# A spectral layer and two MLPs on one core: when weight conversions and low parts are made, and two-bank tiles in the inverse transform

## The chip, the cores and the metric

One core of one Trainium2 chip runs the whole program. The metric is the device time in microseconds (us). The kernel before took 1181.35 us, the median of three runs (1181.19, 1181.35 and 1182.56). Engines are named as in the profile: PE is TensorE, PEld its weight loads, DVE VectorE, ACT ScalarE, POOL GpSimd, SP SyncE.

## The reference

Inputs are `x` (2, 3008, 256) in float32, two 256x256 mixing matrices, two biases, and the float64-valued weights of two MLPs (256 to 2048 to 256).

```python
X = np.fft.rfft(x, axis=1);  Xr, Xi = X.real, X.imag
Yr = Xr @ w_r - Xi @ w_i + b_r
Yi = Xr @ w_i + Xi @ w_r + b_i
Y* = sign(Y*) * max(abs(Y*) - 0.01, 0)          # on Yr and on Yi
y = np.fft.irfft(Yr + 1j*Yi, n=3008, axis=1)    # then reshaped to 6016 tokens
h = y @ w_in;  g = h / (1 + exp(-1.702 h));  y = g @ w_out     # first MLP
h = y @ w_in2; g = h / (1 + exp(-h));        y = g @ w_out2    # second MLP
```

## The kernel before

The program has four stages, told apart on PE: the forward transform (to 67.3 us of the profiled execution), the mixing (to 140.41), the inverse transform (to 197.59) and the MLPs (the rest). The transforms are matmuls with tables that are loaded from HBM (`load_m`, L111); the MLPs are a seven-product scheme with each product in three passes over high and low parts.

**The mixing** has 12 units, one for each (b, p, j), that is batch, half of the spectrum and block of 128 frequencies (`mids`). `mid_mm` (L492) does the matmuls of a unit into two PSUM tiles `psm`, `mid_post` takes the sums, differences and the threshold on DVE and ACT, `mid_fold` makes the tiles `f` (and `fd`) that the inverse reads. Units 0 and 1 (`n32` = 2) are plain float32 matmuls. Units 2 to 11 split both operands in a high and a low part and do 25 matmuls each: for each of eight groups the passes `wh,xh`, `wl,xh`, `wh,xl`, and once the bias. The high part `xh` is a cast on ACT (L480). The low part `xl` is made in two steps (`xsplit`, L468): ACT writes the rounded negative (L476), then POOL issues a DMA that adds the value `xt` to it (L477, 256 KB each, two for a unit). The low parts have 8 buffers and are ordered four units ahead of their use (`xsplit(i + 4, 1)`).

**The weight conversions.** The MLP weights come as 64-bit words. A call of `tick` (L251) moves a chain of blocks on by one: POOL issues an accumulating DMA `cv_a<-cv_c` for the last block's bits (L227); for the block before that, four sums on DVE (L202 to L205, `tmp`), a cast on ACT (L99) and two subtractions on POOL (L100) place it as `wi` (or `wo`, without sums); for a new block, ACT takes the absolute value of `raw` (L165) and DVE does five bit operations (L170 to L174, `cv_c`); then SP loads the next `raw`, which has a single buffer. So L174 of a block is followed by the accumulating DMA, and that by the sums of the same block on DVE, which wait until it has landed. The first ticks stand in the forward loop (`tf`), others in the mixing behind units 2, 6 and 10 (`tm`) and in the inverse behind steps 1, 4, 7 and 10 (`ti`).

**The inverse** has 16 steps (q, b, t), four for each of four output blocks. In `inv_mm` (L567) each step writes two PSUM banks `psi`, one for each half of the channels, taken one by one from the same two pools of four banks that the other stages use. `inv_post` (L600) empties them: for t = 0 and 1, into `rt` (for q = 0 by an ACT copy L611 of one bank and DVE sums L619 and L374, for q = 1 by ACT copies L606), for t = 2 and 3 by a sum into `ac` (L627) and a difference into `rt` (L628), both on DVE. `inv_out` (L636) then combines `ac` and `rt` into the tokens `yt` (L644, L648). `ac` and `rt` have one buffer each.

Engines run their instructions in program order. In nearly all places that order is worked out when the program is built, by a scheduler that looks at dependencies and at due times of its own; only a few engines of some stages keep the order of the code (POOL and SP in the forward transform, SP in the mixing, PE in the inverse).

Of the kernel before, what the change touches and what calls it, by code (L numbers as in the profile page):

```python
# [17 lines left out]
ALU = mybir.AluOpType  # L18
# [38 lines left out]
def spectral_mlp_kernel(ctx, tc, xin, mfwd, minv, wc, bias, w_in1, w_out1, w_in2, w_out2, outT):  # L57
# [408 lines left out]
    xsp = {}  # L466

    def xsplit(i, part):  # L468
        if not N('n32') <= i < len(mids):
            return  # L470
        b, p, j = mids[i]
        for cs in range(2):
            x = xt[b, p, j, cs].rearrange("p q m c -> p (q m c)")
            if part:
# [560 lines left out]
```

## Time and profile before

| | |
|---|---|
| median of three runs | 1181.35 us |
| the profiled execution | 1181.88 us, span 1179.8 us |
| mean granted TensorE clock | 0.998 |
| PE busy | 1157.4 us (98% of the span) |
| ACT, DVE, POOL busy | 761.3, 632.7, 499.9 us |
| stages on PE | forward to 67.3, mixing to 140.4, inverse to 197.6, MLPs to the end |

The profiled execution is 0.53 us above the median. PE is busy in 98% of the span, and the page's slices show the granted clock at nine tenths or more throughout, so what a change can give or cost is in single waits of PE. The view of waits names them, and the timeline of PE says where each stands. Times in rows are microseconds from the start of the span.

### The profile page before, as it was taken

The page shows a single profiled execution, that of the slowest core. Times are in us where ns is not written, and L with a number is a line of the kernel's source. Part 1 is how long each engine was busy: PE and PEld are TensorE (multiplying, and loading weights), DVE is VectorE, ACT ScalarE, POOL GpSimd, SP SyncE. Part 2 cuts the span into 40 slices and gives each one's busy share as a digit, 9 for nine tenths or more (in the row PEclk, how much of TensorE's full clock was granted, in tenths as well). Part 3 has the DMA queues.
Part 4 walks back from the last instruction along what each step waited for, and adds up shares of the span by engine and source line. Part 5 has one row for each costly group of instructions (what it writes and reads, how often), then busy time and mean ns, then how long its engine had stood idle before and what let it go on. Part 6 is the DMA issues. An engine that isn't in the chain of part 4 may idle for free.

```text
span 1179.8 us, 14452 instructions
## 1 busy us (share of the span) xinstructions
PE 1157.4 (98%) x5036; PEld 940.4 (80%) x5036; DVE 632.7 (54%) x976; ACT 761.3 (65%) x1437; POOL 499.9 (42%) x421
## 2 busy tenths in 40 slices
PE   7999989999999999999999999999999999999998
PEld 4758866788888888888889978878888888888897
DVE  7857998666456465565564553432532623524422
ACT  2465633678667667677667776666765765766655
POOL 2353532454444444444436755333333333433333
PEclk9999999999999999999999999999999999999999
DMA  7568332231221221121120100000000000000000
GB/s 267 181 135 229 54 72 54 55 80 28 54 72 36 54 72 28 45 72 37 54 63 28 54 18 19 1 37 1 1 37 1 20 17 1 36 1 1 36 1 32
DMA packets 33610, 61.35 MB, mean 52 GB/s; under 512 B 3073, under 2 KB 12289, under 8 KB 33538
## 3 DMA queue, kind: packets, MB, share of 16 engines
q1 hardware_dynamic: 25730, 46.28, 11.6%
q0 software_dynamic: 7808, 14.16, 6.9%
q8 instruction: 39, 0.64, 0.2%
q14 instruction: 33, 0.27, 0.1%
HBM read 35.92 MB, written 10.35 MB: 39 GB/s over the span
## 4 chain that ended last, share of the span: by engine, by line
PE 72%; ACT 5%; DVE 2%; issue 1%; DMA 0%; POOL 0%; DVEq 0%; ACTq 0%; POOLq 0%
PE o L727 38%; PE x L755 34%; ACT yt L758 2%; ACT g L760 1%; ACT x L674 1%; DVE x L681 1%; ACT yt L774 0%; DVE yt L776 0%; DVE yt L731 0%; DVE yt L797 0%; ACT yt L791 0%; DMA cv_a<-cv_c 0%; ACT yt L789 0%; ACT yt L731 0%; ACT wi L99 0%
## 5 line engine op out<-in xcount | busy, mean ns | idle before, releaser
L765 POOL TENSOR_TENSOR g<-yt,g 128x512 fp32r<-128x512 f32 (+1 forms) x282 | 361.3, 1294 | 531.6 <-PE x L755 364.3
L727 PE MATMUL o<-g,wo 128*128 128x512 f32 (+1 forms) x2304 | 561.0, 386 | 0.9 <-POOL g L765 0.9
L755 PE MATMUL x<-x,wi 128*128 128x512 f32 (+1 forms) x2016 | 501.7, 387 | 5.4 <-ACT yt L791 2.0
L727 PEld LDWEIGHTS o<-g,wo 128*128 128x128 f32 x2304 | 432.4, 188 | 83.6 <-POOL g L765 1.2
L755 PEld LDWEIGHTS x<-x,wi 128*128 128x128 f32 x2016 | 376.0, 188 | 86.0 <-ACT yt L774 5.6
L758 ACT ACTIVATE yt<-yt 128x512 f32<-128x512 f32 (+1 forms) x288 | 179.1, 622 | 257.8 <-DVE yt L797 209.9
L760 ACT CAST g<-yt 128x512 fp32r<-128x512 f32 (+1 forms) x384 | 234.4, 612 | 11.8
L797 DVE TENSOR_TENSOR yt<-yt,x 128x512 f32<-128x512 f32 (+1 forms) x96 | 64.7, 674 | 212.9 <-PE x L755 212.6
L776 DVE TENSOR_TENSOR yt<-yt,x 128x512 f32<-128x512 f32 (+1 forms) x96 | 64.8, 675 | 168.7 <-ACT yt L774 165.9
L765 DVE TENSOR_TENSOR g<-yt,g 128x512 fp32r<-128x512 f32 (+1 forms) x102 | 72.7, 713 | 77.8 <-ACT g L760 77.8
L344 PE MATMUL psf<-m,xf 128*128 128x376 f32 (+2 forms) x208 | 61.1, 456 | 6.4 <-DVE xf L303 6.1
L681 DVE TENSOR_TENSOR x<-yt,x 128x512 fp32r<-128x512 f32 (+1 forms) x46 | 47.8, 1038 | 36.1 <-ACT x L674 36.1
L800 DVE TENSOR_TENSOR yt<-yt,x 128x512 f32<-128x512 f32 (+1 forms) x96 | 64.7, 674 | 0.0
L344 PEld LDWEIGHTS psf<-m,xf 128*128 128x128 f32 x208 | 39.2, 199 | 27.6 <-DVE xf L303 7.3
L774 ACT COPY yt<-x 128x512 f32<-128x512 f32 (+1 forms) x96 | 54.7, 570 | 5.9 <-issue 3.6
L758 ACT ACTIVATE yt<-x 128x512 f32<-128x512 f32 (+1 forms) x96 | 56.1, 584 | 2.1 <-PE x L755 2.1
L344 PE MATMUL psi<-m,f 128*128 128x376 f32 (+3 forms) x208 | 52.1, 406 | 4.3 <-DVE rt L374 4.3
L791 ACT COPY yt<-x 128x512 f32<-128x512 f32 (+1 forms) x96 | 55.8, 581 | 0.8 <-PE x L755 0.8
L789 ACT COPY yt<-x 128x512 f32<-128x512 f32 (+1 forms) x96 | 54.8, 571 | 0.8 <-PE x L755 0.8
L344 PEld LDWEIGHTS psi<-m,f 128*128 128x128 f32 x208 | 37.2, 194 | 17.8 <-DVE rt L374 5.5
L227 POOL DMA_DIRECT2D cv_a<-cv_c x32 | 27.8, 870 | 24.7 <-DVE cv_c L174 14.2
L384 ACT COPY xt<-psf 128x128 f32<-128x128 f32 (+2 forms) x96 | 18.6, 282 | 28.6 <-PE psf L344 28.5
(99 smaller groups left out, 817.8 us busy)
## 6 DMA issues: line engine op xcount, KB each, us to landing
raw<-in_wi SPq DMA_DIRECT2D x32, 256.0 KB, 3.2
cv_a<-cv_c POOLq DMA_DIRECT2D x32, 256.0 KB, 3.3
raw<-in_wo SPq DMA_DIRECT2D x16, 512.0 KB, 3.4
raw<-in_x SPq DMA_DIRECT2D x12, 512.0 KB, 4.8
xl<-xt POOLq DMA_DIRECT2D x20, 256.0 KB, 7.6
out_t<-yt SPq DMA_DIRECT2D x20, 256.0 KB, 2.0
m<-in_mf SPq DMA_DIRECT2D x4, 564.0 KB, 5.3
m<-in_mi SPq DMA_DIRECT2D x4, 564.0 KB, 10.5
```

Of the source, the lines that this page charges most:

```text
L344: nc.tensor.matmul(ps, hi[:, c : c + P], m[:, k, :w], start=i == 0, stop=i == last)
L681: E('xl1' if l else 'xl0' if i == 0 else 'xl', k).tensor_sub(lo, src, r32(hi))
L727: nc.tensor.matmul(acc[h, mm], st, mv, start=first and k == 0, stop=last and k == 2)
L755: nc.tensor.matmul(ps, st, mv, start=first and m == 0, stop=m == 2, skip_group_check=True)
L758: nc.scalar.activation(g, g if src is None else src, func)
L760: nc.scalar.copy(gh, g)
L765: eng.tensor_sub(gl, g, r32(gh))
L776: nc.vector.tensor_add(y1, y1, Y)
L789: nc.scalar.copy(y2, Z)
L791: nc.scalar.copy(y3, X)
L797: nc.vector.tensor_add(y2, y2, X)
L800: nc.vector.tensor_add(y3, y3, Z)
```

## The change

Five things are edited.

1. The ticks of the conversions in the mixing go from behind units 2, 6, 10 to behind units 1, 4, 7, 10; those in the inverse from behind steps 1, 4, 7, 10 to behind steps 2, 5, 8. There are seven of them before and after.
2. The low parts of unit 2, the first one that needs any, are made in the forward loop (group 13) in a pool that is open then.
3. The low parts are ordered three units ahead, not four, and have 6 buffers, not 8. The high parts move into the slots of `xt`.
4. The pool of the placed weights `wi4` and `wi5` is opened before the mixing, not behind it.
5. Each inverse step has one PSUM tile of two banks, out of a pool of four such tiles that takes all eight banks for the inverse; the two pools of four banks are closed before it and opened again behind it. Where one instruction read each half of the channels (L606, L627, L628), one now reads both halves: 16 fewer on DVE, 4 fewer on ACT.

The matmuls are the same in number and shape.

```diff
-'tm': [2, 6, 10], 'ti': [1, 4, 7, 10]
+'tm': [1, 4, 7, 10], 'ti': [2, 5, 8]
...
         if g == 13:
             prep_wc()
+            xsplit(N('n32'), 1, wc_p)
...
+    wib_p.append(opened("wib0", "left", 2))
     wh_p = opened("wh", "left")
-    nh_p = opened("nh", "left", N('nhb'))
+    nh_p = opened("nh", "left", 6)
...
             if part:
-                t = nh_p.tile([P, 512], F32R, tag="lo", name="xl", bufs=8)
+                t = pool.tile([P, 512], F32R, tag="lo", name="xl", bufs=2 if pool is wc_p else None)
                 nc.scalar.mul(t, x, -1.0)
                 nc.gpsimd.dma_start(out=t, in_=x, accum_op=ALU.add)
             else:
-                t = nh_p.tile([P, 512], F32R, tag="hi", name="xh")
+                t = slot(cs, F32R, "xh")
                 nc.scalar.copy(t, x)
...
-    for i in range(N('n32') + 4):
-        xsplit(i, 1)
-        if i < N('n32') + 3:
-            xsplit(i, 0)
+    for i in range(N('n32'), N('n32') + 3):
+        if i > N('n32'):
+            xsplit(i, 1, nh_p)
+        xsplit(i, 0)
     for i in range(len(mids)):
         ps = mid_mm(i)
         if i >= N('n32'):
-            xsplit(i + 4, 1)
+            xsplit(i + 3, 1, nh_p)
             xsplit(i + 3, 0)
...
     closed("mid", "wc", "nh", "wh")
-    wib_p.append(opened("wib0", "left", 2))
...
+    closed("ps1", "ps0")
+    psi_p = opened("psi", bufs=4, space=PS)
...
-        out = [bank(t // 2, "psi") for _ in range(2)]
+        pair = psi_p.tile([P, 2, 512], F32, tag="psi", name="psi")
+        out = [pair[:, x] for x in range(2)]
...
-            for mm in range(2):
-                nc.scalar.copy(row(rt[0], mm, t, n), ps[mm][:, :n])
+            nc.scalar.copy(rows(rt[0], t, n), ps[:, :, :n])
...
-        for mm in range(2):
-            r, a = row(rt[0], mm, t - 2, n), row(ac[0], mm, t - 2, n)
-            nc.vector.tensor_add(a, r, ps[mm][:, :n])
-            nc.vector.tensor_sub(r, r, ps[mm][:, :n])
+        r, a = rows(rt[0], t - 2, n), rows(ac[0], t - 2, n)
+        nc.vector.tensor_add(a, r, ps[:, :, :n])
+        nc.vector.tensor_sub(r, r, ps[:, :, :n])
...
+    closed("psi")
+    ps_p[:] = [opened(f"ps{i}", bufs=4, space=PS) for i in range(2)]
     region('mlp')
```

The order on POOL at the end of the forward transform. Before, one accumulating DMA of the conversions stands behind the bias, then placements, and the eight low parts of units 2 to 5 come last (`xl_654` is unit 2's).

```order
L327 DMA bias_hl_373<-bias_lo_374 1x16x32
L100 TENSOR_TENSOR wi1_776<-cv_a_470,wi1_776 128x384
L227 DMA cv_a_559<-cv_c_558 128x512
L100 TENSOR_TENSOR wi1_776<-tmp_777,wi1_776 128x512
L100 TENSOR_TENSOR wi2_1012<-cv_a_559,wi2_1012 128x384
L100 TENSOR_TENSOR wi2_1012<-tmp_1013,wi2_1012 128x512
L227 DMA cv_a_779<-cv_c_778 128x512
L477 DMA xl_654<-xt0020_100 128x512
L477 DMA xl_657<-xt0021_101 128x512
```

Now the same eight low parts stand directly behind the bias, ahead of the accumulating DMA (the L number of `xl` is 433 now, unit 2's are `xl_600` and `xl_603`).

```order
L327 DMA bias_hl_373<-bias_lo_374 1x16x32
L433 DMA xl_600<-xt0020_100 128x512
L433 DMA xl_603<-xt0021_101 128x512
L433 DMA xl_667<-xt0100_102 128x512
L433 DMA xl_670<-xt0101_103 128x512
L433 DMA xl_677<-xt0110_104 128x512
L433 DMA xl_680<-xt0111_105 128x512
L433 DMA xl_769<-xt0120_106 128x512
L433 DMA xl_772<-xt0121_107 128x512
L227 DMA cv_a_559<-cv_c_558 128x512
```

So the low parts moved ahead of `cv_a_559`, and with it ahead of the sums and placements of that block.

The order on POOL in the mixing. Before, the low parts of unit 6 (`xl_750`, `xl_753`) stand behind the accumulating DMA of the block for `wi4`, `cv_a_1015`, and ahead of the one for `wi5`, `cv_a_1228`.

```order
L100 TENSOR_TENSOR wi3_1225<-tmp_1226,wi3_1225 128x512
L227 DMA cv_a_1015<-cv_c_1014 128x512
L530 TENSOR_TENSOR f0011_836<-th_770 128x512
L477 DMA xl_750<-xt1000_108 128x512
L477 DMA xl_753<-xt1001_109 128x512
L477 DMA xl_824<-xt1010_110 128x512
L477 DMA xl_827<-xt1011_111 128x512
L227 DMA cv_a_1228<-cv_c_1227 128x512
L530 TENSOR_TENSOR f0101_940<-th_896 128x512
```

Now unit 6's low parts (`xl_821`, `xl_824`) stand behind both of these DMAs, `cv_a_902` and `cv_a_1089`, and behind the placement of `wi4`; unit 8's (`xl_947`) come behind a third DMA (`cv_a_1252`, for `wo`), the placement of `wi5`, and the operations `f` and `fd` of the fold.

```order
L227 DMA cv_a_902<-cv_c_901 128x512
L100 TENSOR_TENSOR wi4_1249<-cv_a_902,wi4_1249 128x384
L532 TENSOR_TENSOR f0011_833<-th_789 128x512
L100 TENSOR_TENSOR wi4_1249<-tmp_1250,wi4_1249 128x512
L227 DMA cv_a_1089<-cv_c_1088 128x512
L433 DMA xl_821<-xt1000_108 128x512
L433 DMA xl_824<-xt1001_109 128x512
L100 TENSOR_TENSOR wi5_1389<-cv_a_1089,wi5_1389 128x384
L433 DMA xl_873<-xt1010_110 128x512
L433 DMA xl_876<-xt1011_111 128x512
L227 DMA cv_a_1252<-cv_c_1251 128x512
L100 TENSOR_TENSOR wi5_1389<-tmp_1390,wi5_1389 128x512
```

One more tick of the conversions thus stands ahead of unit 6's low parts than before.

The order on DVE in the inverse, from the emptying of step 3 to that of step 4. Before, three conversion operations (L172 to L174) stand among them.

```order
L627 TENSOR_TENSOR ac_1396<-rt_1346,psi_1387 128x377
L628 TENSOR_TENSOR rt_1346<-rt_1346,psi_1386 128x377
L172 SCALAR_TENSOR_TENSOR cv_a_1424<-raw64_1370,cv_c_1423 128x512
L628 TENSOR_TENSOR rt_1346<-rt_1346,psi_1387 128x377
L648 TENSOR_TENSOR yt_1325<-ac_1396 128x2x377
L644 TENSOR_TENSOR yt_1325<-ac_1396 128x2x376
L173 TENSOR_SCALAR cv_c_1423<-cv_a_1424 128x512
L648 TENSOR_TENSOR yt_1325<-rt_1346 128x2x376
L174 SCALAR_TENSOR_TENSOR cv_c_1423<-raw64_1370,cv_c_1423 128x512
L619 TENSOR_TENSOR rt_1451<-psi_1401,eo_1452 128x2x2x95
L664 TENSOR_TENSOR tmp_1527<-yt_1325 128x512
L374 TENSOR_TENSOR rt_1451<-psi_1401,eo_1452 128x4x94
```

Now none does, and a sum takes both halves of the channels.

```order
L629 TENSOR_TENSOR ac_1418<-rt_1370,psi_1409 128x2x377
L630 TENSOR_TENSOR rt_1370<-rt_1370,psi_1409 128x2x377
L650 TENSOR_TENSOR yt_1351<-ac_1418 128x2x377
L646 TENSOR_TENSOR yt_1351<-ac_1418 128x2x376
L650 TENSOR_TENSOR yt_1351<-rt_1370 128x2x376
L622 TENSOR_TENSOR rt_1446<-psi_1421,eo_1447 128x2x2x95
L666 TENSOR_TENSOR tmp_1526<-yt_1351 128x512
L374 TENSOR_TENSOR rt_1446<-psi_1421,eo_1447 128x4x94
```

The conversion's operations of this stretch moved ahead into the mixing or behind it into later steps.

## Rows read from the trace of the kernel before

**Rows 1.** Waits of PE: engine, line and releaser, total, times, longest.
```profile
PE psi L344 <- DVE rt L374: 4.3, 2, 3.7
...
PE psm L499 <- DMA xl<-xt: 1.5, 1, 1.5
```

**Rows 2.** Timeline of PE, unit 2 of the mixing: start, us, line, count, [idle before].
```profile
81.07 0.80 PE L499 MATMUL psm<-wh,xh 128*128 128x512 f32 x1
...
83.56 0.50 PE L499 MATMUL psm<-wh,xl 128*128 128x512 f32 x1 [1.46 <-DMA xl<-xt]
```

**Rows 3.** Timeline of PE, inverse and start of the MLPs.
```profile
140.41 6.01 PE L344 MATMUL psi<-m,f 128*128 128x192 f32 x36
...
163.71 4.06 PE L344 MATMUL psi<-m,f 128*128 128x376 f32 x12 [0.59 <-DVE rt L374]
171.45 26.59 PE L344 MATMUL psi<-m,f 128*128 128x376 f32 x78 [3.68 <-DVE rt L374]
197.59 2.74 PE L755 MATMUL x<-x,wi 128*128 128x512 f32 x10
```

**Rows 4.** Windows of 2 us: five engines' busy time, PEclk, DMA share, GB/s.
```profile
82.00:84.00 2.00, 0.54 (x3) 0.40 (x3) 1.76 (x4) 2.00 (x6) 2.00 (x3) 1.00 1.11 204
...
172.00:174.00 2.00, 2.00 (x6) 1.09 (x5) 2.00 (x5) 0.00 (x0) 0.00 (x0) 0.60 0.00 0
174.00:176.00 2.00, 2.00 (x5) 1.09 (x4) 2.00 (x4) 0.26 (x1) 0.00 (x0) 0.54 0.00 0
```

**Rows 5.** Timeline of PE's weight loads, the inverse's last stretch at full clock.
```profile
177.98 19.46 PEld L344 LDWEIGHTS psi<-m,f 128*128 128x128 f32 x62
```

**Rows 6.** Timeline of POOL in the mixing.
```profile
59.99 0.55 POOL L327 DMA_DIRECT2D bias_hl<-bias_lo  x1 [1.98 <-DVE bias_lo L326]
...
73.96 0.85 POOL L227 DMA_DIRECT2D cv_a<-cv_c  x1
...
90.74 0.88 POOL L227 DMA_DIRECT2D cv_a<-cv_c  x1 [4.84 <-issue]
...
96.02 0.88 POOL L477 DMA_DIRECT2D xl<-xt  x1 [0.43 <-ACT xl L476]
...
116.41 1.68 POOL L536 TENSOR_TENSOR fd<-f,fb 128x512 f32<-128x512 f32 x1 [5.33 <-DVE fb L530]
```

**Rows 7.** DMA issues in windows from 63, 90.7, 97 and 118 us: KB, us to landing.
```profile
cv_a<-cv_c POOLq DMA_DIRECT2D x1, 256.0 KB, 4.6
...
cv_a<-cv_c POOLq DMA_DIRECT2D x1, 256.0 KB, 6.5
...
xl<-xt POOLq DMA_DIRECT2D x1, 256.0 KB, 10.6
...
xl<-xt POOLq DMA_DIRECT2D x1, 256.0 KB, 3.8
```

**Rows 8.** Timeline of DVE in the mixing.
```profile
81.48 0.29 DVE L202 TENSOR_TENSOR tmp<-cv_a 128x128 f32<-128x128 f32 x1 [5.36 <-DMA cv_a<-cv_c]
...
97.30 0.29 DVE L202 TENSOR_TENSOR tmp<-cv_a 128x128 f32<-128x128 f32 x1 [3.15 <-DMA cv_a<-cv_c]
...
104.03 0.68 DVE L174 SCALAR_TENSOR_TENSOR cv_c<-raw,cv_c 128x512 f32<-128x512 uint32 x1
```

**Rows 9.** Timeline of DVE in the inverse.
```profile
152.16 0.54 DVE L627 TENSOR_TENSOR ac<-rt,psi 128x377 f32<-128x377 f32 x1
...
156.97 0.94 DVE L648 TENSOR_TENSOR yt<-ac 128x754 f32<-128x754 f32 x1
157.82 1.73 DVE L644 TENSOR_TENSOR yt<-ac 128x752 f32<-128x752 f32 x1
...
163.12 0.54 DVE L374 TENSOR_TENSOR rt<-psi,eo 128x376 f32<-128x376 f32 x1
163.57 2.46 DVE L665 TENSOR_TENSOR yt<-yt 128x512 f32<-128x512 f32 x1
...
198.15 0.55 DVE L627 TENSOR_TENSOR ac<-rt,psi 128x376 f32<-128x376 f32 x1 [0.77 <-PE psi L344]
```

More of the change, by code (lines that the diff above doesn't have):

```diff
@@ L420, in spectral_mlp_kernel, with xsplit @@
         fold(g)
+    xsp = {}
+    mids = [(b, p, j) for b in range(B) for p in range(2) for j in range(NJ)]
+    def xsplit(i, part, pool=None):
+        if i >= len(mids):
+            return
+        b, p, j = mids[i]
+        for cs in range(2):
+            x = xt[b, p, j, cs].rearrange("p q m c -> p (q m c)")
+            if part:
+                t = pool.tile([P, 512], F32R, tag="lo", name="xl", bufs=2 if pool is wc_p else None)
+                nc.scalar.mul(t, x, -1.0)
+                nc.gpsimd.dma_start(out=t, in_=x, accum_op=ALU.add)
+            else:
+                t = slot(cs, F32R, "xh")
+                nc.scalar.copy(t, x)
+            xsp[b, p, j, cs, part] = t[:, :].rearrange("p (q m c) -> p q m c", q=2, m=2)
     prev = None
@@ L452, in spectral_mlp_kernel @@
             tick(N('tf').count(g))
-    mids = [(b, p, j) for b in range(B) for p in range(2) for j in range(NJ)]
     closed("xs", "lv", "raw", "m0")
@@ L465, in spectral_mlp_kernel @@
     nc.vector.tensor_sub(wl, wc_s, r32(wh))
[L466 to L474, printed above, removed]
-                t = nh_p.tile([P, 512], F32R, tag="lo", name="xl", bufs=8)
-                nc.scalar.mul(t, x, -1.0)
-                nc.gpsimd.dma_start(out=t, in_=x, accum_op=ALU.add)
-            else:
-                t = nh_p.tile([P, 512], F32R, tag="hi", name="xh")
-                nc.scalar.copy(t, x)
-            xsp[b, p, j, cs, part] = t[:, :].rearrange("p (q m c) -> p q m c", q=2, m=2)
     def mid_mm(i):
@@ L582, in inv_mm @@
                     product(out[eo][:, mm * CU : mm * CU + w], tiles, m, blocks, w, cs * D + mm * P)
-            return out
+            return pair
         for mm in range(2):
@@ L590, in inv_mm, with rows @@
                 product(out[mm][:, :188], tiles, m, ((1 - cs, 2), (2, 3)), 188, c)
-        return out
+        return pair
     rt, ac = {}, {}
     RW = 2 * 378
-    def row(x, mm, t, n):
-        return x[:, t * RW + mm * 378 : t * RW + mm * 378 + n]
+    def rows(x, t, n):
+        return x[:, t * RW : (t + 1) * RW].rearrange("p (m c) -> p m c", m=2)[:, :, :n]
     def inv_post(q, b, t, ps):
@@ L609, in inv_post @@
             w = mshape("i", q, 0)[1]
-            ev, od = by_half(ps[0]), by_half(iv_p.tile([P, 2 * CU], F32, tag="eo", name="eo", bufs=N("eob")))
-            nc.scalar.copy(od[:, :, :w], by_half(ps[1])[:, :, :w])
+            ev, od = by_half(ps[:, 0]), by_half(iv_p.tile([P, 2 * CU], F32, tag="eo", name="eo", bufs=N("eob")))
+            nc.scalar.copy(od[:, :, :w], by_half(ps[:, 1])[:, :, :w])
             add, sub = nc.vector.tensor_add, diff(t)
```

2 lines of the change are left out of this document (1 added, 1 removed).

## The prediction

> **What bounds the kernel now.** The page's first part has PE busy in 98% of the span, so a change that keeps the matmuls moves the time by the waits of PE alone. I read the view of waits first: two entries lie where the change works, 4.3 us on DVE's `rt` in the inverse and 1.5 us on a low part in the mixing [rows 1]. PE's timeline then shows the places: unit 2's first `wh,xl` waits 1.46 us [rows 2], step 8 of the inverse 0.59 us and step 9 3.68 us [rows 3]. The windows show what comes behind the last one: the granted clock is 0.60 and 0.54 from 172 to 176 us, which is the 1.2 GHz level for most of it, while around the shorter wait in the mixing it was 1.00 [rows 4]. From 177.98 on 62 weight loads take 19.58 us to the MLPs' first matmul, 0.316 each; the 16 ahead of them took 177.98 - 171.45 = 6.53 us where 16 x 0.316 = 5.05 would do, so the slow clock cost 1.5 us [rows 3, 5]. All that can be won here is therefore 1.46 + 0.59 + 3.68 + 1.5 = 7.2 us.
>
> **Unit 2.** Its low parts are made in the forward stage and are the first DMAs behind the bias on POOL, at about 60.5 [rows 6]. They land by 71.1 even at the longest landing here, 10.6 [rows 7], and PE wants them at 81.07 + 0.49 [rows 2]. The 1.46 us go.
>
> **The inverse.** Step 9 waited for step 5's L374, step 8 for step 4's, which ended at 163.66, 23.25 us behind the inverse's start at 140.41 [rows 3, 9]. In the new order no conversion stands on DVE before it. The walk: step 3 ends 10.24 us into the inverse (64 records of 0.16); its sum and difference over both halves take about 1.9 (four operations of 0.54 at 0.46 spacing, as L627 [rows 9]); `inv_out` 0.94 + 1.73 + 0.94, the middle one blocked as before [rows 9]; then L622, L666 and L374, 0.54 + 0.68 + 0.54. That ends at about 17.5. Step 8 begins 20.5 us in if nothing waits, so 3 us are to spare. Step 9, at 24.3, needs step 6's difference on the two-bank tile; behind L374 stand L667 (up to 2.46 [rows 9]) and six operations of 0.5 to 0.94, which end at 24 to 24.6. I take 0.3 us of wait. The two-bank tile has a price: before, the first half of steps 8 and 9 could start alone in a bank that was free, now both halves wait, up to 2.0 us of early start each; with 3 us to spare it isn't called on. So 4.27 - 0.3 are won, and with the wait the 1.5 of slow clock. The 20 instructions saved lie on DVE and ACT, which PE waits for at these two places only, and are in the walk already.
>
> **The start of the MLPs.** The pools of four banks are opened again over the two-bank tiles, so the MLPs' third group of banks, `x_1621`, lies on step 15's tile and waits for its last DVE operation, L630. Before, the same place held a bank that had been read long ago. Step 15's first sum started at 198.15, held by the last matmul [rows 9]; two operations over both halves, 0.92 and 1.0, end at 200.07. PE gets there at 197.59 + 3 x 0.23 = 198.28 [rows 3]. That is a new wait of 1.8 us; from nothing, if PE's later groups are late anyway, to 2.1.
>
> **The chain in the mixing.** Here the move of POOL's queue counts. Eight low parts now stand ahead of `wi2`'s accumulating DMA: 60.5 + 8 x 0.88 = 67.6 [rows 6]. It lands 4.6 to 10.6 later [rows 7]; I take 76. The sums and bit operations that follow end with L174 of the next block at about 78.3, so that `wi3`'s DMA goes out at 78.6 where it went at 73.96 [rows 6]. Then the chain runs as before: landing 4.6 [rows 7], at 83.2; 13 operations of 0.28 to 0.68 on DVE, 5.5, to 88.7; `wi4`'s DMA, 6.5 [rows 7], at 95.4; again 5.1 (the same stretch took 97.30 to 104.71 before, with three more operations in it [rows 8]), to 100.5, where L174 of `wi5`'s block ends. DVE stood in this chain before too: it waited 5.36 and 3.15 us for the landings [rows 8]. What is new is who is queued behind it. On POOL, unit 6's low parts now stand behind the DMA that waits for this L174. Before, they went out at 96.02 [rows 6], and the longest landing was still in time; now they go out at 101.4. At the same L174 SP issues the next `raw` (512 KB) and four tables of 564 KB, so the landing is nearer to 10.6 than to the 3.8 of quiet time [rows 7]; I take 8, and the low part is there at 109.4. PE wants it at 81.56 + 4 x 5.73 = 104.5 (248 matmuls from 83.56 to 140.41 are 0.229 each, 25 to a unit [rows 2, 3]). It waits 4.9 us.
>
> Unit 7's come 5 us later on both sides and add nothing. Unit 8's stand behind `wi5`'s landing (7.4 behind L174, with the issue), ten operations of DVE (4.6), a cast (0.6), three operations of POOL at 1.68 (`fd` [rows 6]; 5.0) and their own landing (3.8 [rows 7]): 100.5 + 21.4 = 121.9, against 81.56 + 6 x 5.73 = 115.9. The delay in all is thus 6.0 us, of which 1.1 comes at unit 8. From there on landings are short and the chain pauses. A wait of 4.9 us is longer than the one behind which the clock fell, so I put another 1.5 us to it.
>
> Both ends: with landings of 3.8 to 4.6 throughout, L174 ends at 96.7, unit 6's parts are there at 101.4 and nothing waits but 0.3 at unit 8. With L174 at 104.7, where the block's L174 ended before [rows 8], and 10.6 of landing, unit 6 waits 11.8 us.
>
> On such a DMA the Trainium skill has a rule ("DMA: Bandwidth & Descriptors", Anatomy of one DMA): one issued by GpSimd takes about 2.0 us and the bytes over 436 GB/s. As an estimate from that page, 256 KB would take 2.6 us, the chain would be 5 us ahead of my walk, and the new waits in the mixing would be gone; the time would be the first rival's. The trace speaks against it: 3.8 us is the shortest of the landings here and 10.6 the longest [rows 7].
>
> **The sum.** - 1.46 - 4.27 - 1.5 + 0.3 + 1.8 + 6.0 + 1.5 = + 2.4 us on the profiled execution's 1181.88, so 1184.3; it lies 0.53 above the median, which gives 1183.7. What can be told from no change is 0.2%, 2.4 us, so the forecast stands at that bound: 56% for it, from 1181 to 1187, by delays in the mixing from 4 to 9 us; 0.34 of this above the bound and 0.22 within.
>
> **Rivals.**
> First, the low parts land in time. The price of the mixing is 0 to 0.3 and no clock falls there: - 5.1, 1176.3; with the MLPs' wait absorbed as well, 1174.5. It decides at L174 of `wi5`'s block: it must end before 104.5 less issue and landing, 104.5 - 0.9 - 5 = 98.6. For it: POOL's issues from 118 us on land in 3.8, and unit 2's early low parts take load off the queues at 76 to 83. Against it: 1.9 us have to be found in a chain of three landings. 24%, faster.
> Second, the waits are there but short, 2 to 4 us, and the clock holds, as it did around 1.46 us: - 5.2 + 3 = - 2.2, 1179. 12%, half faster and half the same.
> Third, the inverse keeps its wait: DVE is behind by more than 3 us at step 4, since `rt` and `ac` have one buffer and the mixing's last sums come late; then the two-bank tile takes the early half steps away and the 5.8 us stay: 1183.7 + 5.5, 1189. In the trace DVE is busy through all of 160 to 176; without the conversions it has room. 8%, slower.
>
> So faster 0.24 + 0.06 = 0.30, the same 0.22 + 0.06 = 0.28, slower 0.34 + 0.08 = 0.42. The range goes from the first rival's time to between the forecast's upper end and the third's: 1176.3 to 1188.
>
> **What would show it.** Right: no wait on `xl` at unit 2; one of 4 to 6 us at unit 6 with POOL's issue behind `cv_a_1089` at 101 or later, and DVE waiting for `cv_a` before it; no wait on L374 and a clock of 1.00 in the inverse; a wait of 1.8 on L630 at the MLPs' second group of matmuls. Wrong: an `xl` issue for unit 6 before 98.6, or landings near 4 us there; a wait in the inverse of over 1 us; a first MLP group that doesn't wait.

## The result and the profile after

The changed kernel takes 1193.38 us, the median of four runs (1191.06 to 1194.19); the kernel before, run beside it on the same chip, takes 1181.27 (four runs, 1179.53 to 1182.56). The ratio is 1.010, with a 95% interval from 1.0085 to 1.0116: about 1% slower. The prediction was 1183.7 with a range to 1188.0, so the time lies outside. The profiled execution took 1191.06 us (span 1189.3, granted clock 0.994); it is the fastest of the four, so 2.3 us of the median are in no trace.

| on PE, us | before | after | difference |
|---|---|---|---|
| start to unit 2 of the mixing | 81.07 | 80.44 | -0.63 |
| unit 2 to the inverse | 59.34 | 71.85 | +12.51 |
| inverse | 57.18 | 52.50 | -4.68 |
| MLPs to the end of the span | 982.2 | 984.5 | +2.3 |
| span | 1179.8 | 1189.3 | +9.5 |

The waits of PE (engine, line and releaser; total, times, longest), where [rows 1] stood before:

```profile
PE psm L501 <- DMA xl<-xt: 12.4, 1, 12.4
...
PE psi L344 <- issue: 1.6, 1, 1.6
...
PE x L759 <- DVE rt L630: 1.5, 1, 1.5
```

The 4.3 us on L374 have gone and 1.6 us of another wait stand in their place; the low parts have one wait as before, but of 12.4 us and not of 1.5. PE's timeline has the places:

```profile
80.44 0.80 PE L501 MATMUL psm<-wh,xh 128*128 128x512 f32 x1
...
116.77 0.80 PE L501 MATMUL psm<-wh,xl 128*128 128x512 f32 x1 [12.41 <-DMA xl<-xt]
117.37 0.63 PE L501 MATMUL psm<-wh,xh 128*128 128x512 f32 x1
117.79 0.63 PE L501 MATMUL psm<-wl,xh 128*128 128x512 f32 x1
...
152.29 6.01 PE L344 MATMUL psi<-m,f 128*128 128x192 f32 x36
178.47 26.77 PE L344 MATMUL psi<-m,f 128*128 128x376 f32 x84 [1.57 <-issue]
204.79 1.16 PE L759 MATMUL x<-x,wi 128*128 128x512 f32 x3
207.41 3.67 PE L759 MATMUL x<-x,wi 128*128 128x512 f32 x15 [1.46 <-DVE rt L630]
```

Unit 2 no longer waits [rows 2]; the 12.41 us stand at unit 6, whose first `wh,xl` was due at 104.36. Matmuls then come 0.42 apart where 0.23 is usual. The windows (five engines' busy time, PEclk, DMA share, GB/s) show this clock, and the one of the inverse:

```profile
106.00:108.00 2.00, 0.00 (x0) 0.00 (x0) 1.81 (x4) 0.88 (x2) 2.00 (x3) 0.61 0.73 197
108.00:110.00 2.00, 0.00 (x0) 0.00 (x0) 0.00 (x0) 0.62 (x2) 0.41 (x1) 0.50 1.01 287
...
118.00:120.00 2.00, 2.00 (x6) 1.52 (x6) 2.00 (x6) 1.69 (x3) 0.49 (x1) 0.50 1.10 253
120.00:122.00 2.00, 2.00 (x10) 1.65 (x9) 1.97 (x2) 1.85 (x5) 1.71 (x2) 0.98 1.09 252
...
176.00:178.00 2.00, 0.90 (x3) 0.19 (x1) 2.00 (x4) 1.05 (x3) 0.00 (x0) 1.00 0.00 0
178.00:180.00 2.00, 1.53 (x5) 1.06 (x6) 2.00 (x5) 0.61 (x2) 0.00 (x0) 1.00 0.00 0
```

PE stands idle, the clock falls to 0.50, which is the 1.2 GHz level, and stays there until 120; in the inverse it is 1.00 around its wait of 1.57 us and behind it, where it was 0.60 and 0.54 behind the wait of before [rows 4]. The mixing's 12.51 us are thus - 1.46 (unit 2) + 12.41, and a remainder of 1.56, which I put down to the slow clock: at 0.42 for 0.23 from 116.77 to about 120.25 it makes as much.

What led to the wait stands on three engines. On DVE, from the landing of `wi3`'s DMA to the end of L174 of `wi5`'s block:

```profile
83.91 0.29 DVE L202 TENSOR_TENSOR tmp<-cv_a 128x128 f32<-128x128 f32 x1 [3.91 <-DMA cv_a<-cv_c]
...
84.93 1.11 DVE L204 TENSOR_TENSOR tmp<-tmp,cv_a 128x128 f32<-128x128 f32 x1
...
87.44 1.78 DVE L172 SCALAR_TENSOR_TENSOR cv_a<-raw,cv_c 128x512 uint32<-128x512 uint32 x1
...
90.79 0.69 DVE L174 SCALAR_TENSOR_TENSOR cv_c<-raw,cv_c 128x512 f32<-128x512 uint32 x1
...
98.21 0.29 DVE L202 TENSOR_TENSOR tmp<-cv_a 128x128 f32<-128x128 f32 x1 [3.25 <-DMA cv_a<-cv_c]
...
98.96 1.11 DVE L204 TENSOR_TENSOR tmp<-tmp,cv_a 128x128 f32<-128x128 f32 x1
99.99 1.51 DVE L171 TENSOR_SCALAR cv_c<-cv_c 128x512 uint32<-128x512 uint32 x1
101.42 0.28 DVE L205 TENSOR_TENSOR tmp<-cv_a,tmp 128x128 f32<-128x128 f32 x1
101.62 0.68 DVE L172 SCALAR_TENSOR_TENSOR cv_a<-raw,cv_c 128x512 uint32<-128x512 uint32 x1
102.22 0.68 DVE L513 TENSOR_TENSOR sd<-us,psm 128x512 f32<-128x512 f32 x1
...
104.54 0.68 DVE L174 SCALAR_TENSOR_TENSOR cv_c<-raw,cv_c 128x512 f32<-128x512 uint32 x1
```

On POOL and on ACT:

```profile
84.85 1.04 POOL L100 TENSOR_TENSOR wi<-cv_a,wi 128x384 fp32r<-128x384 f32 x1 [3.58 <-ACT wi L99]
87.31 1.36 POOL L100 TENSOR_TENSOR wi<-tmp,wi 128x512 fp32r<-128x512 f32 x1 [1.42 <-ACT wi L99]
92.37 0.88 POOL L227 DMA_DIRECT2D cv_a<-cv_c  x1 [3.70 <-issue]
98.75 1.17 POOL L100 TENSOR_TENSOR wi<-cv_a,wi 128x384 fp32r<-128x384 f32 x1 [5.50 <-DVE tmp L203]
99.89 1.33 POOL L532 TENSOR_TENSOR f<-th 128x512 f32<-128x512 f32 x1
...
105.75 0.88 POOL L227 DMA_DIRECT2D cv_a<-cv_c  x1 [2.02 <-issue]
106.33 2.07 POOL L433 DMA_DIRECT2D xl<-xt  x2
```

```profile
101.73 0.62 ACT L99 CAST wi<-tmp 128x512 fp32r<-128x512 f32 x1 [3.07 <-DVE tmp L205]
102.93 1.39 ACT L519 ACTIVATE th<-sd,neglam 128x512 f32<-128x512 f32 x2 [0.58 <-DVE sd L513]
104.23 0.56 ACT L511 COPY us<-psm 128x512 f32<-128x512 f32 x1
104.69 0.63 ACT L432 ACTIVATE xl<-xt 128x512 fp32r<-128x512 f32 x1
```

Read backwards: the low part leaves POOL at 106.33, behind the DMA that waited for L174 (104.54 + 0.68 = 105.22). But ACT wrote it only at 104.69, behind `th`, which needed the `sd` of 102.22 on DVE, which stood behind sums that waited 3.25 us for a landing. So the low part is late on ACT too: its write ends at 105.32 (104.69 + 0.63), and POOL's order alone can have held it for 1 us at most. From 106.33 it lands in 10.4 us (to 116.77), among the tables. The DMA issues from 106 to 108.5 us (KB each, us to landing; for two the later one's):

```profile
m<-in_mi SPq DMA_DIRECT2D x4, 564.0 KB, 9.5
xl<-xt POOLq DMA_DIRECT2D x2, 256.0 KB, 11.8
```

ACT's waits in the mixing (76 to 150 us) have two kinds that the kernel before did not have there, for the placing's landings and for the slots of the high parts:

```profile
ACT wi L99 <- DMA cv_a<-cv_c: 6.7, 3, 3.3
...
ACT xh L436 <- DMA xl<-xt: 1.4, 2, 1.3
```

### The profile page after: what moved, and what is told of

It reads as the page before. It is cut to its first block, busy times and chain, and to the rows that moved or that the text cites. A ratio compares the mean times of both kernels' runs of the same rounds, so it can differ in the third digit from the quotient of the medians.

```text
span 1189.3 us, 14431 instructions
## 1 busy us (share of the span) xinstructions
PE 1155.7 (97%) x5036; PEld 939.9 (79%) x5036; DVE 631.9 (53%) x960; ACT 761.2 (64%) x1433; POOL 498.9 (42%) x421
## 4 chain that ended last, share of the span: by engine, by line
PE 82%; ACT 5%; DMA 5%; DVE 4%; issue 3%; POOL 1%; SPq 0%; DVEq 0%; POOLq 0%; ACTq 0%
PE o L731 39%; PE x L759 34%; PE psi L344 4%; PE psm L501 3%; DMA cv_a<-cv_c 3%; PE psf L344 2%; ACT yt L762 2%; ACT g L764 1%; DMA raw<-in_x 1%; DMA xl<-xt 1%; DVE lv L292 1%; DVE x L683 0%; ACT yt L778 0%; ACT x L676 0%; POOL g L769 0%
## 5 line engine op out<-in xcount | busy, mean ns | idle before, releaser
L764 ACT CAST g<-yt 128x512 fp32r<-128x512 f32 (+1 forms) x384 | 234.4, 612 | 11.8
L501 PE MATMUL psm<-wh,xl 128*128 128x512 f32 x80 | 31.9, 399 | 12.4 <-DMA xl<-xt 12.4
L227 POOL DMA_DIRECT2D cv_a<-cv_c x32 | 30.5, 952 | 23.0 <-DVE cv_c L174 15.8
```

The source lines that it names most:

```text
L501: nc.tensor.matmul(t, st, mv, start=n == 0 and k == 0, stop=n == 3 and grp == 1 and k == 2)
L764: nc.scalar.copy(gh, g)
```

## The experiments

Each was timed against the kernel before on its own chip; a ratio has its 95% interval in brackets. Where medians of different chips are set side by side, the ratios say what holds.

**Number of ticks, queues, load.** The first four start from the changed kernel.

```diff
-'tm': [1, 4, 7, 10], 'ti': [2, 5, 8]
+'tm': [2, 6, 10], 'ti': [1, 4, 7, 10]
```

> The changed kernel with the ticks of the conversions put back to units 2, 6, 10 and steps 1, 4, 7, 10; all else as changed. On POOL unit 6's low parts still stand behind the accumulating DMAs for wi4 and wi5. Theory of the queue (the wait comes from what stands ahead of the low parts on POOL): unit 6 still waits 8 to 14 us for its low part, time 1187 to 1195. Rival of the extra tick (a fourth conversion in the mixing is too much for DVE and the queues): the wait is gone, time 1175 to 1180.

Measured: 1191.29, 1.0102 [1.0087, 1.0117]; 11.2 us of waits on low parts. The wait is 10.5 us at unit 6 and 0.6 at unit 8, nearly the same. So the places of the ticks in the code do not make it. It does not follow that fewer conversions in the mixing would not help: POOL issues five `cv_a` DMAs from 76 to 150 us in this run (80.15 to 136.41), as in the changed kernel (79.07 to 133.03), where the kernel before has two (90.74 and 105.26). The scheduler draws the conversions ahead into the mixing in both, wherever their ticks stand in the code.

```diff
-'mid': 'SP'
+'mid': 'Pool,SP'      # POOL, too, keeps the code's order in the mixing
```

> The changed kernel with POOL kept in the order of the code in the mixing, so that the low parts of units 5 to 8 stand ahead of the next accumulating DMAs; ticks, pools and tiles as changed. Theory of the queue: no wait on a low part over 1 us at unit 6 or later, no fall of the clock there, about 14 us less than the changed kernel: 1176 to 1180, faster than before. Rival of the load (the low parts land late because tables and raw weights fill the DMA queues at that time, wherever they stand): 4 us of wait or more stay, time 1183 or more.

Measured: 1195.67, 1.0135 [1.0117, 1.0153], a miss. No low part is waited for, but PE waits at the inverse's start:

```profile
150.57 4.82 PE L344 MATMUL psi<-m,f 128*128 128x192 f32 x14 [11.24 <-ACT th L519]
```

The conversions now come late, DVE falls behind, and the wait is moved.

```diff
+'li': [3, 4, 5, 6]    # units behind which the inverse's tables are loaded
```

> The changed kernel with the inverse's tables ordered behind units 3, 4, 5, 6 in place of 5, 6, 7, 8, so that the two large ones (2.3 MB) go out one tick earlier and not at the same L174 as unit 6's low parts. POOL's order around unit 6 is the same. Theory of the queue with the load as a second term: the issue stays at 105 to 109, the landing falls from 10.4 to 4 to 6 us, so unit 6 waits 7 to 11 us in place of 12.4, time 2 to 6 us under the changed kernel. If load plays no part: landing and wait as in the changed kernel, 12 us.

Measured: 1193.21, 1.0119 [1.0098, 1.014]; 12.6 us of waits on low parts. Now `wi4`'s DMA meets the tables, DVE waits 5.61 us for it, and the low part goes out at 113.11: the load moves to an earlier link of the chain.

```diff
+            with tc.issue_after(ahead[8]) if i == 10 else ExitStack():   # POOL: behind unit 8's low parts
+                tick(N('tm').count(i))
```

> The changed kernel with one constraint of order more: on POOL the accumulating DMA for wi5 and all of that tick come behind the low parts of unit 8. So the low parts of units 6, 7 and 8 are issued when their own inputs are ready and not behind L174 of wi5's block; nothing else is edited, and the inverse has the same order as in the changed kernel. Theory of the queue: no wait over 2 us on a low part, no fall of the clock in the mixing; the inverse waits 1 to 3 us, the MLPs 1.5 us: 12 to 15 us less than the changed kernel, 1177 to 1181. Rival of the moved chain (as in the run with the whole order of the code, the conversions come later and the wait goes into the inverse): a wait of 4 us or more at the start of the inverse or in it, 1184 or more.

Measured: 1192.55, 1.0092 [1.0075, 1.0109]; the wait is 8.3 us. POOL stands idle for 7.41 us until ACT has written the low part, as read above:

```profile
104.65 0.88 POOL L433 DMA_DIRECT2D xl<-xt  x1 [7.41 <-ACT xl L432]
```

Of the 4.1 us that are gone, 1.7 are the earlier issue (104.65 for 106.33) and 2.1 a shorter landing; PE comes to it 0.35 later. The earlier issue is not POOL's order alone either: ACT writes the low part 1 us earlier here, since on DVE, with POOL idle, these two are not held (below):

```profile
99.90 0.29 DVE L204 TENSOR_TENSOR tmp<-tmp,cv_a 128x128 f32<-128x128 f32 x1
100.10 0.42 DVE L171 TENSOR_SCALAR cv_c<-cv_c 128x512 uint32<-128x512 uint32 x1
```

**The early placing of `wi4`.** Two runs hold the last conversion of the mixing behind unit 6's `sd` on DVE and behind unit 8's low parts on ACT and POOL; the second loads the tables early as well.

```diff
+            with ExitStack() as late:
+                for k in (("sd", 6), 8, ("mul", 8)) if i == 10 else ():
+                    late.enter_context(tc.issue_after(ahead[k]))
+                tick(N('tm').count(i))
...
+'li': [3, 4, 5, 6]    # in the second run only
```

> The changed kernel, but the fourth conversion of the mixing (wi4's sums on VectorE, its cast on ScalarE, GpSimd's half-subtraction and the loads of the next block) stands behind unit 6's difference on VectorE, and behind unit 8's low parts on ScalarE and GpSimd. Theory (VectorE waits in order for the landing of wi4's accumulating DMA, 3.25 us, ahead of the mixing's own sums, and th and the low parts come behind that): no VectorE wait for that landing before unit 6, unit 8's low part issued at about 98 us and not 106.33, unit 6's difference landing counted 8 to 10 us later: TensorE waits 2 to 4 us at most in unit 8 and nothing in unit 6; 8 to 10 us below the changed kernel, 1181 to 1185, if the conversion has room at the mixing's end; a wait of 3 to 10 us at the inverse's start if it has not. Rival (the landing among the tables' loads alone makes the wait): the low part still lands at 113 or later, wait 8 or more, 1189 or more.

> As the run with the fourth conversion placed late, and the inverse's tables loaded at units 3 to 6, so that they do not stand in the DMA queues beside unit 8's low part. Theory (order on VectorE, ScalarE and GpSimd decides, load second): low part issued at about 98, landing 4 to 5, TensorE waits 0 to 2 us in the mixing; 1178 to 1182. Rival (the load only moves): a landing of 8 us or more at an earlier unit with a wait there of 3 us or more, 1185 or more.

Measured: 1192.75, 1.0096 [1.0078, 1.0113], with waits of 7.8 on low parts and 3.6 at the inverse; and 1193.54, 1.01 [1.0084, 1.0117], with 10.0 and 3.6. Both missed. The wait for `wi4`'s landing is gone from DVE, but DVE and ACT then wait 1.3 to 2.2 us for the next `raw`, and the low part of unit 6 still leaves at 103.00 and 107.82 and lands 9.2 and 5.8 us later.

Two runs keep the unit 2 edit, the high parts in the slots of `xt` and the two-bank tile, and go back to the ticks of before with the pool behind the mixing; with its memory the first has a lead of four, the second of three.

```diff
-    wib_p.append(opened("wib0", "left", 2))
-    nh_p = opened("nh", "left", 6)
+    nh_p = opened("nh", "left", 8)                 # first run only
...
-            xsplit(i + 3, 1, nh_p)
+            xsplit(i + 4, 1, nh_p)                 # first run only
...
     closed("mid", "wc", "nh", "wh")
+    wib_p.append(opened("wib0", "left", 2))
```

> The changed kernel with the pool of wi4 and wi5 opened behind the mixing, the old ticks, and low parts four units ahead in 8 buffers; unit 2's early low parts and the two-bank tiles stay. On POOL unit 6's low parts are now ahead of both late accumulating DMAs, unit 7's stand behind the one for wi5. Theory of the queue: no wait at units 2 and 6; unit 7's are issued at 105 to 107, land 5 to 10 us later and are wanted at 110: a wait of 1 to 7 us at unit 7, and in the inverse 3 to 5 us as with the two-bank tiles alone: 1182 to 1189. Rival (the extra low parts made early are themselves the load): unit 6 or an earlier one waits.

> As the run before it, but with low parts three units ahead in 6 buffers as in the changed kernel. On POOL unit 6's low parts stand behind both accumulating DMAs, for wi4 and wi5, though no placement of wi4 stands ahead of them. Theory of the queue: unit 6 waits 8 to 13 us as in the changed kernel, time 1190 to 1198. Rival (the early pool and the placement of wi4 in the mixing are what holds POOL): the wait is under 4 us.

Measured: 1192.54, 1.0091 [1.0072, 1.011], no wait on low parts, but 1.8 us on a high part and 3.7, 3.3 and 1.7 us in the inverse; and 1187.63, 1.0052 [1.0032, 1.0073], with 2.3 on low parts, 1.2 on a high part and 6.2 in the inverse. With the pool late the mixing's wait all but goes, yet neither run comes back to the time of before. Something else of the change still costs.

The second of these and the run with the ticks of before differ in one thing, the place where the pool is opened. With lead, slots and tile alike, the early pool has 11.2 us of waits on low parts, and the late one 2.3. So in this kernel the early pool makes some 9 us of the mixing's wait. With the late pool about 5 us of it stand in the inverse instead (7.6 us of waits on `psi` against 2.4), which is why the time falls by less. The two runs with the late pool differ in the lead and its buffers alone, and the longer lead is not the faster: with eight buffers ACT waits 8.8 us for the slots of the high parts, with six it has no such wait.

**The lead.** With the early pool, as I reckoned and no run shows, no memory is left for eight low parts. But units 6 and 10 can reuse the two tiles of unit 2:

```diff
-                t = pool.tile([P, 512], F32R, tag="lo", name="xl", bufs=2 if pool is wc_p else None)
+                t = (wc_p if i % 4 == 2 else pool).tile([P, 512], F32R, tag="lo", name="xl", bufs=2 if i % 4 == 2 else None)
...
-            xsplit(i + 3, 1, nh_p)
+            xsplit(i + 4, 1, nh_p)
```

> The changed kernel with the low parts made four units ahead again: units 6 and 10 reuse the two tiles that unit 2's low parts had, so that no more memory is needed; early pool, four conversions in the mixing and all else as changed. Theory A (the lead: with three units VectorE's, ScalarE's and GpSimd's delays of 10 us and more reach TensorE, with four they are covered): unit 6's low part is issued before 98 us, no wait over 2 us in the mixing, unit 2 to inverse 59 to 61 us, total 1177 to 1181, below the kernel before. Theory B (the early fourth conversion takes VectorE's time wherever the low parts stand): the wait moves to unit 7 or to the inverse's start, 6 us or more in all, 1187 or more.

Measured: 1190.22, 1.008 [1.0067, 1.0094]; waits of 2.17 us at unit 6, 5.13 and 0.59 at unit 7. Theory A fails in this kernel, and ACT shows why:

```profile
100.45 0.52 ACT L99 CAST wi<-cv_a 128x384 fp32r<-128x384 f32 x1 [2.78 <-DMA cv_a<-cv_c]
100.87 1.15 ACT L432 ACTIVATE xl<-xt 128x512 fp32r<-128x512 f32 x2
```

Unit 6's low part was ordered a unit earlier, but stands on ACT behind the cast of the early placing, which waits for a landing. The same question was put to the kernel before, with the unit 2 edit and the inverse's conversions held (below). The first of two runs has six buffers, so that unit 6's tile comes free with unit 3; the second has the tiles reused:

```diff
-                t = (pool or pools["nh"]).tile([P, 512], F32R, tag="lo", name="xl", bufs=2 if pool else 6)
+                t = (wc_p if i % 4 == 2 else pools["nh"]).tile([P, 512], F32R, tag="lo", name="xl", bufs=2 if i % 4 == 2 else 6)
```

> The kernel before with two edits: the low parts of unit 2 made before the mixing in two tiles of their own (the change's edit that took the 1.46 us wait away) and the inverse's conversions held behind the step's own subtraction on VectorE (as in the run with the inverse pinned); the lead becomes three units for unit 6 on. Theory A (a lead of three makes the wait): the mixing waits 3 us or more for a low part, 1181 or more. Theory B (the early pool and its fourth conversion make it, the lead alone is enough): no wait over 1 us in the mixing, 1175 to 1178.

> The kernel with unit 2's low parts before the mixing and the inverse's conversions held, and a lead of four units again (units 6 and 10 reuse unit 2's two tiles); it differs from the run before it, which waited 6.0 us, in the lead alone. Theory (the lead decides that wait): no wait over 1 us in the mixing, some 8 us less than that run with its slow clock, 1175 to 1178; rival (GpSimd's, ScalarE's and VectorE's order in the mixing decides): 3 us or more of wait stay, 1181 or more.

Measured: 1185.22, 1.0033 [1.0021, 1.0046], and 1178.5, 0.9992 [0.9983, 1.0002]. POOL and PE of the first:

```profile
105.00 0.88 POOL L227 DMA_DIRECT2D cv_a<-cv_c  x1 [8.75 <-DVE cv_c L174]
105.58 2.08 POOL L433 DMA_DIRECT2D xl<-xt  x2
...
110.87 0.80 PE L500 MATMUL psm<-wh,xl 128*128 128x512 f32 x1 [6.01 <-DMA xl<-xt]
```

and of the second:

```profile
96.01 0.88 POOL L433 DMA_DIRECT2D xl<-xt  x1 [0.73 <-ACT xl L432]
...
104.85 0.50 PE L500 MATMUL psm<-wh,xl 128*128 128x512 f32 x1 [0.30 <-DMA xl<-xt]
```

They differ in the lead alone, and it moves the low part by 9.6 us across the conversion's DMA, and the wait from 6.01 to 0.8 in all. So a lead of three makes such a wait by itself, with no early pool. How long it is hangs on the landing as well: in the run with the late pool and the lead of three above, unit 6's part goes out as late (105.12), lands in 3.3 us and not in 5.3, and the wait is 2.29.

Then the lead of four (the diff above with `xsplit(i + 4, 1, nh_p)`) and the late placing together, on the changed kernel:

```diff
+            xsplit(i + 4, 1, nh_p)
...
+                for k in (("sd", 6), 8, ("mul", 8)) if i == 10 else ():
+                    late.enter_context(tc.issue_after(ahead[k]))
```

> The changed kernel with a lead of four units and with the fourth conversion of the mixing held behind unit 6's difference and unit 8's low parts: both suspected causes are gone. Theory (the two together make the 12.4 us): waits of 0 to 2 us in the mixing, 1178 to 1184, or as much as that with a wait of 2 to 4 us at the inverse's start. Rival (a third cause, such as VectorE's work as a whole): 5 us or more in the mixing, 1188 or more.

Measured: 1189.96, 1.0091 [1.0077, 1.0105]; 3.59 us at unit 7 and 5.26 at the inverse's start. The time is the rival's, so the two causes together do not account for it, though the wait in the mixing lies between the theory's 2 us and the rival's 5. ACT's waits in this run point to a third, 9.4 us on casts of high parts that wait for low parts' landings.

**The high parts in the slots of `xt`.** The kernel of 1178.5 with one line changed:

```diff
-                t = pools["nh"].tile([P, 512], F32R, tag="hi", name="xh")
+                t = slot(cs, F32R, "xh")
```

> The kernel with unit 2's low parts early, a lead of four and the inverse's conversions held (1178.5, waits of 0.8 us in the mixing), with the high parts in the slots of xt, as the change has them, and in nothing else different. Theory (a cast into such a slot must wait on ScalarE until the low part's DMA has read the xt in it, and th and the next low part stand behind it): ScalarE waits 3 to 10 us for xl landings in the mixing, TensorE 1 to 4 us for xh or xl; 1180 to 1185. Rival (the early pool alone makes what is left with a lead of four): no wait of TensorE over 1 us in the mixing, 1177 to 1179.5.

Measured: 1188.92, 1.0068 [1.0053, 1.0083], more than expected. PE waits 1.9 us on a high part in the mixing and 1.0 on low parts there. ACT's waits from 76 to 150 us and PE's waits in the inverse:

```profile
ACT xh L436 <- DMA xl<-xt: 8.4, 6, 3.1
```

```profile
154.45 0.59 PE L344 MATMUL psi<-m,fd 128*128 128x190 f32 x2 [1.28 <-DVE sd L514]
...
160.32 6.49 PE L344 MATMUL psi<-m,f 128*128 128x192 f32 x28 [3.02 <-DVE rt L374]
```

Without the edit ACT has no such wait. A slot is free only when the DMA that reads its `xt` is done; ACT waits there in order, `th` comes late, and DVE is behind when the inverse starts. This one line costs 0.0076 of the time, 9 us, in this kernel, which has a lead of four. With a lead of three ACT's waits for slots are far shorter (1.4 us in the changed kernel, none in the run with the late pool), so this price cannot be carried over to the changed kernel.

**The inverse and the two-bank tile.**

The tile alone, on the kernel before:

```diff
-        out = [bank(t // 2, "psi") for _ in range(2)]
+        pair = psi_p.tile([P, 2, 512], F32, tag="psi", name="psi")
+        out = [pair[:, x] for x in range(2)]
```

> The kernel before with the two-bank tiles of the inverse alone. My account: the conversions stay on DVE in the inverse, so L374 of steps 4 and 5 ends as late as before, and steps 8 and 9 can no longer begin one half early: waits of 4 to 9 us in the inverse, and 1.5 us more at the start of the MLPs for step 15's last operation: 1182 to 1188. Rival (the two-bank tiles and their fewer instructions are what took the waits out of the inverse): waits in the inverse of 2 us or less, clock at 1.00, time 1175 to 1180.

Measured: 1185.38, 1.0045 [1.0031, 1.006]; a step waits 3.47 us and the MLPs' start 1.46. The trace is of the fastest run, 1181.41, and the inverse's waits in it are no longer than before (4.0 us against 4.3), so most of the median's loss is in no trace. The same lines on the kernel of 1178.5:

> The same kernel (1178.5) with the change's two-bank tile in the inverse and in nothing else different. Theory (the tile takes 20 instructions from VectorE and ScalarE, but a step can no longer start in one free bank, and the MLPs' first group waits for the last step's banks): no waits within the inverse since the conversions are held, the wait of 3.0 us at the MLPs' second block 1 to 2 us shorter, a new one of 1.5 at their start: 1177 to 1179.5. Rival (the tile costs, as it did alone: 4 us): 1181 or more, with a wait of 2 us or more in the inverse.

Measured: 1181.71, 1.002 [1.001, 1.003], the rival. The step that waits:

```profile
164.91 32.25 PE L344 MATMUL psi<-m,f 128*128 128x376 f32 x96 [3.43 <-issue]
```

The tile costs in both kernels, by the ratios. I take it that a step can no longer start in the one bank that is free, but this is argued: the wait here ends 0.1 us behind step 4's L374 (164.27 + 0.54), which stands 24.6 us into the inverse, 2.1 us later than in the kernel without the tile. Only the rest, about 1.3 us, can be the missing early half.

The inverse's conversions held, on the kernel before:

```diff
-'ti': [1, 4, 7, 10]
+'ti': [1, 8, 10, 12]      # second run only
...
-                    tick(N('ti').count(step))
+                    with tc.issue_after(done[0]) if step > 1 else ExitStack():   # done[0]: the step's L628
+                        tick(N('ti').count(step))
```

> The kernel before, with the conversions of the inverse's steps 4, 7 and 10 held behind the subtraction on VectorE that ends the step's own result, so that the scheduler cannot pull them ahead; nothing of the change is in it. Theory (the inverse's waits of before, 0.59 and 3.68 us with some 2 us of slow clock, come from the order of VectorE alone and need neither the two-bank tile nor fewer conversions): both waits under 1 us, 5 to 6 us less, 1175 to 1177. Rival (VectorE's total work in the inverse decides, so that only fewer conversions or half the instructions help): waits of 3 us or more stay, 1180 or more.

> As the run with the inverse's conversions held, and at steps 8, 10 and 12 for 4, 7 and 10, so that VectorE has none between the first adding-up at step 4 and step 8. Theory (order of VectorE): TensorE waits under 0.5 us in the inverse, but the last conversion ends later and the MLP's first block may wait 1 to 2 us for it; 1174 to 1178. Rival (total work): waits of 2 us or more in steps 8 to 12 or 3 us or more at the MLPs' start, 1180 or more.

Measured: 1178.57, 0.9975 [0.9963, 0.9988], and 1182.27, 1.0002 [0.9992, 1.0012]. The first is 1.6 us above its theory's range. All waits in the inverse are gone with nothing of the change in it: the order on DVE made them. The first run's inverse takes 50.7 us. But the MLPs wait for a late conversion, 5.6 us in the second run and in the first:

```profile
201.59 0.96 PE L756 MATMUL x<-x,wi 128*128 128x512 f32 x3 [2.94 <-DVE yt L777]
```

Last, on the kernel of 1178.5:

```diff
-'ti': [1, 4, 7, 10]
+'ti': [1, 4, 7, 15]
```

> The kernel with unit 2's low parts early, a lead of four and the inverse's conversions held (1178.5), with the last conversion of the inverse at step 15 in place of step 10. Theory (the 3.0 us at the MLPs' second block come from the conversion's 3.6 us on VectorE ahead of the last sums): that wait is under 1 us, total 1175 to 1177. Rival (VectorE has no room there and the conversion delays the MLPs' first blocks instead): 2 us or more of waits on yt or wo after 198 us, 1178 or more.

Measured: 1179.87, 0.9997 [0.9984, 1.0009]. That wait falls to 1.3, but those on POOL's `g` grow from 0.8 to 1.9. The only run whose interval lies wholly below the kernel before is the one with the inverse's conversions held and nothing else, by 0.25%.

## Why the prediction was wrong

**Unit 2: right.** No wait is left (- 1.46).

**The inverse: right in kind.** L374's wait and the slow clock went. I left 0.3 us at step 9 and it is 1.57, which is over the 1 us that I had named as a sign of being wrong. The walk was short here: step 4's L374 ends 19.0 us into the inverse and not 17.5, one more `inv_out` operation being held, and a conversion's L172 (176.84) still stands in front of L630, behind whose end, 178.37, step 9 starts 0.1 later:

```profile
177.45 0.92 DVE L630 TENSOR_TENSOR rt<-rt,psi 128x754 f32<-128x754 f32 x1
```

Of the tile's price I had written that it isn't called on. Step 9 does wait for both halves, but how much of the 1.57 a free first bank would have saved no run shows. The stage gained 4.68 where my terms make 4.27 + 1.5 - 0.3 = 5.47. The third rival did not come, and the runs with the conversions held show that the gain needed neither tile nor fewer conversions.

**The MLPs' start: right.** 1.46 against 1.8. The stage is 2.3 longer; beside this wait only 0.3 us on `g` is found, and the rest is not traced to waits.

**The chain in the mixing: the step that failed.** I had 6.0 us of delay at units 6 and 8; it is 12.41, all at unit 6, and 0.6 above even my upper bound of 11.8. Link by link, walk against trace: `wi2` lands at 76 both times; `wi3`'s DMA goes out at 78.6 and at 79.07; DVE's first stretch takes 5.5 against 7.6 (83.91 to 91.48); `wi4`'s DMA goes out at 88.9 against 92.37; the second stretch takes 5.1 against 7.0 (98.21 to 105.22); L174 ends at 100.5 against 105.22; the low part leaves at 101.4 against 106.33 and takes 8 against 10.4. So 4.9 us are of the walk and 2.4 of the landing. With the clock the mixing's new waits cost 13.97 us where the sum has 6.0 + 1.5.

Of the two stretches, 4.0 us too short, 3.9 are four operations on DVE that ran beside a POOL operation and ended 0.15 to 0.55 us behind it: L204 twice 1.11, where L205 of the same shape takes 0.28, L172 1.78 against 0.68, and L171 1.51 against 0.41 (at 86.50). I had taken the free durations, though [rows 9] had a blocked one that I did use in the inverse. The Trainium skill states a rule for it ("SBUF — State Buffer", Who interferes with whom): an operation of VectorE with two inputs in SBUF and one of GpSimd that reads SBUF share a port pair, and the later one is held until the earlier is done. The trace agrees for L204 and L172, which have two inputs: L204 begins at 84.93 beside the L100 of 84.85 to 85.89 and ends at 86.04. L171 has one input, so the rule as told does not reach it; it was held all the same (1.51 from 99.99, beside the L532 of 99.89 to 101.22, and 0.42 in the run where POOL was idle).

The first two rivals fell with this term: the low part missed its time by 12 us, and the clock did not hold.

**What the step left out.** It told the wait as a matter of POOL's order alone. With the low part ahead in POOL's order 8.3 us remained, because ACT, too, comes to it late: there it wrote it at 103.72, with nothing held on DVE in the second stretch, where the walk had it leave at 101.4. And it gave no price to two edits, each of which costs in some other kernel: the lead of three (6.0 us of wait in a kernel with nothing of the early pool) and the high parts in the slots (9 us in a kernel with a lead of four). The early pool itself it priced by its eight low parts ahead and one landing; in the pair that differs in it alone it makes some 9 us of wait, with conversions drawn ahead into the mixing. I had named the lead in the description and let the walk stand on the queue; of the slots I wrote nothing.

**What is not settled.** How the 12.41 us divide among the lead, the early placing and the slots: the parts don't add up (the runs with a lead of four and with late placing have 1190 to 1193), and in the changed kernel itself ACT waits only 1.4 us for slots but 6.7 for landings of `cv_a`. In the pair with three units of lead, slots and tile, the early pool is most of it; for the changed kernel's own ticks and for other leads no run has the pool alone. The early pool without the slots was not tried. I reckoned that the memory does not hold both, so that the early pool forces that edit and the shorter lead; no run shows this.

## What to carry to other kernels

When a change buys room in memory, price what it is paid with: a shorter lead or a shared slot turns transfers that were hidden into waits of in-order engines, and one such wait delays all that the engine has queued. Follow a late transfer back through every engine that prepares it, not only the queue that issues it. And where one edit removes a wait, look first whether the order of the instructions alone does it: here that took all waits out of the inverse with nothing paid for room, though 2.9 us of wait came at the MLPs' start and 0.25% was left of it. And price such edits together, not one by one: the longer lead was worth 0.4% in one kernel and cost 0.4% in another, where the slots had to wait for it.

## What the runs showed of the hardware

Accumulating DMAs of 256 KB that POOL issues took from 3.2 to 12.6 us to land; the first of the forward stage, behind eight low parts, 12.6 (63.43 to 76.0, of which 3.55 are the issue itself). From the end of L174 on DVE to the issue on POOL that waits for it 0.5 to 0.9 us pass. After its long wait of 12.41 us PE ran at the 1.2 GHz level for 3.5 us, and that cost 1.56 us as the remainder of the stage, hardly more than the 1.5 behind a wait of 3.68 us before.
